# A fused transformer block: products ahead of the transposes, weights in chunks, gated dummy matmuls, and TensorE's branch behind its last matmul

## The chip, the cores and the metric

The kernel runs on one core of one Trainium2 chip. The metric is the device time of one execution in microseconds. The span of a profile (first to last instruction) is some 1.7 us shorter than that time. All executions here scatter by about 1 us, as much as the effects in question, so most comparisons rest on five executions of a kernel and on the runs of the kernel before that were taken beside them on the same chip.

## The reference

```python
mod = (silu(c) @ w_mod).reshape(c.shape[0], 6, 1, -1)        # c: 1x512, w_mod: 512x3072
sa, ca, ga, sb, cb, gb = (mod[:, i] for i in range(6))
h = layernorm(x) * (1 + ca) + sa                              # x: 1x2048x512
x = x + ga * attention(h, k_cache, v_cache, wq, wo)           # 32 heads of 128, 8 kv heads, last 512 keys
h = layernorm(x) * (1 + cb) + sb
x = x + gb * (relu(h @ w1) @ w2)                              # 512 -> 1792 -> 512
```

The rows are worked in four blocks of 512. Before the first score matmul the kernel needs the first block normalized, transposed, scaled with `1 + ca` and shifted with `sa`, and projected to queries.

## The kernel before

The start, cut to what the change touches. The dummy matmuls (`warm`) produce nothing that is used; they are meant to bring TensorE's clock up. In the trace of before the clock is read from spacing: its dummies start 427 ns apart, and 512-column matmuls in the body 216 ns (508 to 513 us). The first is called half clock here.

```python
    for i in range(2):                                   # x: two halves, one per queue
        dma(x_sb[:, 2 * i:2 * i + 2, :], ..., eng=ACT if i else SP)
    dma(c_row[:, :], ...)
    load_wm01(0)                                         # modulation weights: two halves of 512 KB
    load_wm01(1, ACT)
    load_wq(0, 2, ACT)                                   # query weights, heads 0 and 1
    load_wq(2, 2)
    load_k(0)
    load_v(0)
    ...
    warm(7)                                              # dummies, 128x512
    silu_exp(5)                                          # transpose of c on TensorE, exp on ScalarE
    warm(9)
    ...                                                  # statistics of row tile 3 on ScalarE
    silu_mul()                                           # GpSimd: 1/(1+exp(-c)), times c
    ln_stat(0); ln_stat(1); rstd_add(0, 2); rstd_pow(0, 2)    # powers on GpSimd
    ln_stat(2); rstd_add(2, 3); rstd_pow(2, 4)
    ln_norm(0); ln_norm(1)                               # VectorE
    ...                                                  # row tile 3 normalized on GpSimd, after the powers
    ln_tposes(0, TB[0])                                  # 4 transposes of row tile 0
    for f in mod_cols_mm(0, QBK): f()                    # the 32 products with one column
    ln_norm(2)
    mod_cols_evac(0, QBK)                                # modc, on VectorE
    for tl in range(1, TPB):
        ln_tposes(tl, TB[tl // 2])
    ...                                                  # scale and shift, first projections
```

The end. A flag, computed at about 478 us, tells whether a general version of the kernel must be run instead. Each engine loads it and branches at its own place; TensorE does so before two of the groups of the second MLP product:

```python
                mlp.insert(len(mlp) - 2, lambda: cut_here("pe"))
    ...
                kb.emit(stream, e, 0, n_ops)             # n_ops: the cut
                e.wait_ge(sems[flag_ev[0]], flag_ev[1])
                v = e.value_load(flag[0:1, 0:1])
                with e.If(v != 128):
                    ...                                  # rest of the fast version, then the general version
                with e.Else():
                    kb.emit(stream, e, n_ops)            # rest of the fast version
```

## Time and profile before

| | before |
|---|---|
| time, median of the first three runs | 560.52 us (560.2 to 560.57) |
| span of the profile | 559.4 us |
| TensorE busy | 98% |
| transpose of c | 4.94 us |
| products | 9.04 to 9.98 us |
| first projection | 10.86 us |
| first scores (first record at 13.34; the one ahead of it has none) | about 13.12 us |
| TensorE's branch | 510.64 to 514.08 us |
| last matmul's start to the end of the span | 2.89 us |

The profiled execution took 561.1 us, 0.6 us more than that median.

Busy time by engine, from the first part of the page, gives the frame: no engine but TensorE is near its limit.

```profile
PE 550.5 (98%) x4060; PEld 315.8 (56%) x4134; DVE 253.8 (45%) x551; ACT 348.9 (62%) x453; POOL 54.7 (10%) x53
```

### The profile page before, as it was taken

To read this page: it belongs to the slowest core of one execution; us is meant where nothing else is said; L and a number is where in the kernel's file an instruction comes from. 1 tells how busy PE (TensorE), PEld (TensorE's weight loads), DVE (VectorE), ACT (ScalarE), POOL (GpSimd) and SP (SyncE) were. 2 spreads that over 40 slices of the span, in tenths; PEclk is the share of its full clock that TensorE was granted. 3 is DMA by queue.
4 is the path that set the end of the run, shared out by engine and by line. 5 is a ranking of instruction groups with operands and counts; after the bars stand their busy time and mean duration, and the time that the engine had idled before them with its cause. 6 is when DMAs were issued, how large, how long until landed. Compare 5 with 4: busy or idle time off the path is not lost.

```text
span 559.4 us, 9666 instructions
## 1 busy us (share of the span) xinstructions
PE 550.5 (98%) x4060; PEld 315.8 (56%) x4134; DVE 253.8 (45%) x551; ACT 348.9 (62%) x453; POOL 54.7 (10%) x53
## 2 busy tenths in 40 slices
PE   8999999999999999999999999999999999999998
PEld 4665555555555555555555555555555654444444
DVE  4455555553546544335445443333354448321134
ACT  4986666666666666666666666666666644432500
POOL 3000022004410000033000000332000000000000
DMA  9897763513114144352352412111215110210001
GB/s 268 248 207 174 143 169 46 114 39 76 40 38 76 39 73 117 58 133 57 94 95 57 76 40 39 39 39 38 39 39 76 39 30 0 44 34 23 22 29 47
DMA packets 113309, 42.67 MB, mean 76 GB/s; under 512 B 93928, under 2 KB 112104, under 8 KB 113256
## 3 DMA queue, kind: packets, MB, share of 16 engines
q1 hardware_dynamic: 112024, 40.82, 34.3%
q10 hardware_dynamic: 1232, 1.15, 0.6%
q8 instruction: 33, 0.54, 0.4%
q14 instruction: 20, 0.16, 0.1%
HBM read 18.35 MB, written 2.10 MB: 37 GB/s over the span
## 4 chain that ended last, share of the span: by engine, by line
PE 98%; issue 1%; DMA 1%; DVE 0%; SPq 0%; DVEq 0%
PE psS L1372 28%; PE psO L1372 27%; PE psQ L1372 23%; PE psW L1372 20%; DMA c_row<-in_c_dram 1%; DVE qT L1611 0%; DVE hT L1630 0%; SPq L1303 0%; DVE PT L1723 0%; DVE PT L1725 0%; PE psS L1375 0%; PE psO L1416 0%; DVE modc L1438 0%; DVEq L123 0%
## 5 line engine op out<-in xcount | busy, mean ns | idle before, releaser
L1493 ACT ACTIVATE PT<-psS 128x1024 bf16<-128x1024 f32 x256 | 262.7, 1028 | 128.2 <-PE psS L1372 128.1
L1372 PE MATMUL psS<-qT,kT 128*128 128x512 bf16 x508 | 150.9, 379 | 0.5 <-DVE qT L1611 0.4
L1372 PEld LDWEIGHTS psO<-v,PT 128*128 128x128 bf16 x2048 | 126.6, 98 | 30.2
L1372 PE MATMUL psO<-v,PT 128*128 128x129 bf16 x2048 | 137.0, 220 | 0.0
L1372 PE MATMUL psQ<-hT,wq 128*128 128x512 bf16 (+1 forms) x510 | 130.5, 377 | 0.3 <-DVE hT L1630 0.2
L1503 DVE RECIPROCAL rinv<-psO 128x4 f32<-128x4 f32 x128 | 23.3, 182 | 227.2 <-PE psO L1372 227.2
L1372 PE MATMUL psW<-wo,oT 128*128 128x512 bf16 x454 | 118.1, 379 | 3.0
L1504 DVE TENSOR_TENSOR o<-psO,rinv 128x512 bf16<-128x512 f32 x128 | 88.5, 691 | 4.9 <-DVE rinv L1503 0.5
L1372 PEld LDWEIGHTS psQ<-hT,wq 128*128 128x128 bf16 x512 | 49.9, 98 | 60.3 <-issue 0.6
L1372 PEld LDWEIGHTS psS<-qT,kT 128*128 128x128 bf16 x512 | 49.5, 98 | 58.9 <-ACT PT L1493 0.7
L1485 ACT ACTIVATE qT<-psQ 128x512 bf16<-128x512 f32 x126 | 74.7, 593 | 0.0
L1712 ACT ACTIVATE wq<-psS 128x512 bf16<-128x512 f32 x56 | 33.4, 597 | 49.3 <-PE psS L1372 48.9
L1372 PEld LDWEIGHTS psW<-wo,oT 128*128 128x128 bf16 x512 | 45.0, 98 | 32.9 <-DVE acc L1526 1.2
L1526 DVE TENSOR_TENSOR acc<-psW,acc 128x512 f32<-128x512 f32 x48 | 33.2, 691 | 6.5 <-PE psW L1372 6.5
L1372 PE MATMUL psO<-wmw,wq 128*128 128x512 bf16 (+1 forms) x165 | 32.8, 352 | 0.3
L1529 POOL TENSOR_TENSOR acc<-acc,gaf 128x512 f32<-128x512 f32 x12 | 15.6, 1303 | 146.7 <-DVE acc L1526 139.8
L1388 POOL TENSOR_TENSOR rstd<-rstd,cst 128x4 f32<-128x4 f32 x7 | 7.2, 1025 | 216.8 <-DVE rstd L1387 216.8
L1723 DVE TENSOR_TENSOR PT<-psO,gbf 128x512 f32<-128x512 f32 (+1 forms) x12 | 7.5, 624 | 40.4 <-PE psO L1372 40.4
L1372 PE MATMUL psS<-h2T,wmw 128*128 128x512 bf16 x109 | 25.0, 379 | 0.2
L1372 PEld LDWEIGHTS psO<-wmw,wq 128*128 128x128 bf16 x168 | 15.3, 98 | 16.5
L1372 PE MATMUL psS<-hT,wmw 128*128 128x512 bf16 x110 | 24.4, 379 | 0.1
L1382 DVE BATCH_NORM_STATS2 st<-x 128x6 f32<-128x512 bf16 x31 | 21.1, 681 | 4.8 <-DMA x<-in_A_x_dram 4.8
(85 smaller groups left out, 192.6 us busy)
## 6 DMA issues: line engine op xcount, KB each, us to landing
wo<-in_A_wo_dram SPq DMA_DIRECT2D x4, 1024.0 KB, 5.9
wq<-in_A_wq_dram SPq DMA_DIRECT2D x7, 512.0 KB, 4.6
wmw<-in_B_w_dram SPq DMA_DIRECT2D x14, 256.0 KB, 3.1
wmw<-in_w_mod_dram SPq DMA_DIRECT2D x5, 512.0 KB, 4.8
oT<-o SPq DMA_TRANSPOSE x128, 2.4
out_dram<-PT SPq DMA_DIRECT2D x15, 128.0 KB, 1.7
x<-in_A_x_dram SPq DMA_DIRECT2D x3, 512.0 KB, 4.3
v<-in_A_v_cache_dram SPq DMA_DIRECT2D x8, 128.0 KB, 3.8
```

The costliest lines, as they stand in the source:

```text
L1372: kb.op(PE, lambda e: e.matmul(out_ap, lhsT, rhs, start=start, stop=stop), reads=reads, group_writes=[R_b[k] for k in bk], signal=signal)
L1382: kb.op(DVE, lambda e: e.bn_stats(st[:, t, :], x_sb[:, t, :]), reads=[R_x[t]], writes=[R_st[t]])
L1388: kb.op(POOL, lambda e: e.tensor_tensor(rstd[:, sl], rstd[:, sl], cst[:, 0:1].to_broadcast([P, hi - lo]), op=ALU.pow), reads=R_rstd[sl] + ...
L1485: kb.op(ACT, lambda e: e.activation(qT[u % NQT][:, :], bank[bk], ACTF.Copy), reads=[R_b[bk]], writes=[R_qT[u % NQT]])
L1493: kb.op(ACT, lambda e: e.activation(PT[u % NPT][:, pr * 2:pr * 2 + 2, :], s_ps[pr][:, :, :], ACTF.Exp, scale=scale), reads=[R_b[pr * 2], R ...
L1503: kb.op(DVE, lambda e: e.reciprocal(rinv[:, u, :], o_ps[:, :, P]), reads=[R_b[5], R_b[6]], writes=[R_rinv])
L1504: kb.op(DVE, lambda e: e.tensor_tensor(o_sb[u % NOS][:, :, :], o_ps[:, :, 0:P], rinv[:, u, :].unsqueeze(2).to_broadcast([P, TPB, P]), op=A ...
L1526: kb.op(DVE, lambda e: e.tensor_tensor(acc[:, tl, :], bank[WBK], acc[:, tl, :], op=ALU.add), reads=[R_b[WBK], R_acc[tl]], writes=[R_acc[tl]])
L1529: kb.op(eng, lambda e: e.tensor_tensor(acc[:, tl, :], acc[:, tl, :], gaf[:, :], op=ALU.mult), reads=[R_acc[tl], R_ga], writes=[R_acc[tl]])
L1712: kb.op(ACT, lambda e: e.activation(h1T[b % 2][:, fc, :], bank[bk], ACTF.Relu), reads=[R_b[bk]], writes=[R_h1[b % 2][fc]], pre=all_events( ...
L1723: kb.op(DVE, lambda e: e.tensor_tensor(yt[i][:, c0:c1], bank[bk][:, c0:c1], gbf[:, c0:c1], op=ALU.mult), reads=[R_b[bk], R_gb], writes=[R_ ...
```

## The change

The intent: run the 32 products as soon as silu(c) is there, ahead of all transposes; let their weights come in the order of use; replace nine dummies, which hold TensorE back until 8.8 us, with a few that wait for events; and save TensorE's stall at the branch by taking the branch when TensorE has nothing left to do. The diff, cut to its core:

```diff
-        c0, c1 = i * DC // 2, (i + 1) * DC // 2
-        dma(wm01[:, c0:c1, :], wm01v[:, c0:c1, :], f"wm{i}", writes=[R_wm[i]], eng=eng)
+        dma(wm01[:, i, :], wm01v[:, i, :], f"wmc{i}", writes=[R_wmc[i]], eng=eng)
...
-    load_wm01(0)
-    load_wm01(1, ACT)
-    load_wq(0, 2, ACT)
+    for i in range(DC):
+        load_wm01(i, (ACT, SP)[i % 2])
+    for i, eng in enumerate((SP, SP)):
+        dma(wq_sb[:, 2 * i:2 * i + 2, 0:QA * Dh], ..., f"wqa{i}", writes=[R_wqa[i]], eng=eng)
+    load_k(0)
     load_wq(2, 2)
-    load_k(0)
     load_v(0)
-    kb.op(POOL, lambda e: e.memset(ones[:, :], 1.0), writes=[R_ones])
+    kb.op(DVE, lambda e: e.memset(ones[:, :], 1.0), writes=[R_ones])
...
-    warm(7)
+    warm(10)
     silu_exp(5)
-    warm(9)
...
     ln_stat(0)
+    warm(3, [R_mv[0]])
     ln_stat(1)
+    warm(2, [R_mv[1]])
...
-    ln_tposes(0, TB[0])
     fs = mod_cols_mm(0, QBK)
     for f in fs:
         f()
+    ln_tposes(0, TB[0])
+    mod_cols_evac(0, QBK)
     ln_norm(2)
-    mod_cols_evac(0, QBK)
...
-    for tl in range(1, TPB):
-        ln_tposes(tl, TB[tl // 2])
+    ln_tposes(1, TB[0])
+    warm(2, bk=6)
+    ln_tposes(2, TB[1])
+    ln_tposes(3, TB[1])
+    warm(1, bk=6)
...
-                mlp.insert(len(mlp) - 2, lambda: cut_here("pe"))
...
+    cut_here("pe")
```

More of the change, by code (lines that the diff above doesn't have):

```diff
@@ L1319, in build_fast @@
     R_q1 = RL("q1_", 2)
+    R_wmc = RL("wmc", DC)
+    R_wqa = RL("wqa", 2)
     R_cf, R_m01 = Res("cf"), Res("m01")
@@ L1350, in load_wm01 @@
     def load_wm01(i, eng=None):
-        c0, c1 = i * DC // 2, (i + 1) * DC // 2
-        dma(wm01[:, c0:c1, :], wm01v[:, c0:c1, :], f"wm{i}", writes=[R_wm[i]], eng=eng)
+        dma(wm01[:, i, :], wm01v[:, i, :], f"wmc{i}", writes=[R_wmc[i]], eng=eng)
     def wm_res(sl, cc):
-        return R_wm[cc // (DC // 2)] if sl < 2 else R_wm[sl]
+        return R_wmc[cc] if sl < 2 else R_wm[sl]
     def load_wo(j):
@@ L1363, in load_mlp @@
         if not wm_done:
-            wm_done.extend(all_events(R_wm))
+            wm_done.extend(all_events(R_wm + R_wmc))
         f0 = i % (FC // 2) * 2
@@ L1375, in tpose, with warm @@
         kb.op(PE, lambda e: e.transpose(out_ap, in_ap, ident[:, :]), reads=list(reads) + [R_ident], group_writes=[R_b[k] for k in bk], signal=signal)
-    def warm(n):
+    def warm(n, gate=(), bk=7):
         for i in range(n):
-            mm(bank[WBK], ones[:, :], ones[:, 0:1].to_broadcast([P, QB]), True, True, [R_ones], [WBK], i == n - 1)
+            mm(bank[bk], ones[:, :], ones[:, 0:1].to_broadcast([P, QB]), True, True, [R_ones] + list(gate), [bk], i == n - 1)
     def ln_stat(t):
@@ L1480, in q_mms @@
             mm(bank[bk], wq_sb[:, cc, h * Dh:(h + 1) * Dh], hT[b % 2][:, cc, :], i == 0, i == DC - 1,
-               [R_wq[h], R_hT[b % 2][cc]] + ([R_h0[cc]] if b == 0 else []), [bk], i == DC - 1)
+               (R_wqa if h < QA else [R_wq[h]]) + [R_hT[b % 2][cc]] + ([R_h0[cc]] if b == 0 else []), [bk], i == DC - 1)
         q_evac(u, bk)
@@ L1561, in build_fast @@
     dma(c_row[:, :], c[0].rearrange("(c p) -> c p", p=P), "c", writes=[R_c])
-    load_wm01(0)
-    load_wm01(1, ACT)
-    load_wq(0, 2, ACT)
+    for i in range(DC):
+        load_wm01(i, (ACT, SP)[i % 2])
+    for i, eng in enumerate((SP, SP)):
+        dma(wq_sb[:, 2 * i:2 * i + 2, 0:QA * Dh], wqv[:, 2 * i:2 * i + 2, 0:QA * Dh], f"wqa{i}", writes=[R_wqa[i]], eng=eng)
+    load_k(0)
     load_wq(2, 2)
-    load_k(0)
     load_v(0)
-    kb.op(POOL, lambda e: e.memset(ones[:, :], 1.0), writes=[R_ones])
+    kb.op(DVE, lambda e: e.memset(ones[:, :], 1.0), writes=[R_ones])
     kb.op(POOL, lambda e: e.memset(cst[:, 0:1], -0.5), writes=[R_cst])
@@ L1636, in q_half @@
             mm(bank[bk][:, hf * HB:(hf + 1) * HB], wq_sb[:, cc, u * Dh:(u + 1) * Dh], hT[0][:, cc, hf * HB:(hf + 1) * HB], cc == CC_ORDER[0], cc == CC_ORDER[-1],
-               [R_wq[u], R_half[hf][cc]], [bk], cc == CC_ORDER[-1])
-    for tl in range(1, TPB):
-        ln_tposes(tl, TB[tl // 2])
+               [R_wqa[cc // 2], R_half[hf][cc]], [bk], cc == CC_ORDER[-1])
+    ln_tposes(1, TB[0])
[3 more added lines that the diff above has]
+    warm(1, bk=6)
     mod_half(0, 0, DVE)
@@ L1712, in h1_group @@
         kb.op(ACT, lambda e: e.activation(h1T[b % 2][:, fc, :], bank[bk], ACTF.Relu), reads=[R_b[bk]], writes=[R_h1[b % 2][fc]],
-              pre=all_events(R_wq) if b < 2 else ())
+              pre=all_events(R_wq + R_wqa) if b < 2 else ())
     def y_group(b, tl, c0=0, c1=D, deng=None):
```

## The prediction

> **What bounds the kernel now.** I read three views in this order. First the shares by engine of the chain that ended last, for the whole span:
>
> ```profile
> PE 98%; issue 1%; DMA 1%; DVE 0%; SPq 0%; DVEq 0%
> ```
>
> TensorE is the path for all but some 2% of 559.4 us, so nothing that shortens work on another engine in the body of the kernel can help. What is left is where TensorE is on the path without useful work, or waits: the first 13 us, and single stalls. So second, the same chain in order of time for the first 14 us (start, us, what):
>
> ```profile
> 1.24 3.66 DMA c_row<-in_c_dram
> 4.90 0.05 issue
> 4.95 0.18 PE psO L1416
> 5.13 3.86 PE psW L1372 x9
> 8.98 0.22 PE psS L1375 x4
> 9.21 0.79 PE psQ L1372 x32
> 10.00 0.02 issue
> 10.02 0.18 DVE modc L1438
> ...
> 10.30 0.42 DVE hT L1630
> ...
> 10.86 0.78 PE psQ L1372 x4
> 11.64 0.89 PE psO L1372 x8
> ...
> 12.55 0.44 DVE qT L1611
> ```
>
> The reader is to see the third to fifth PE pieces: nine dummy matmuls hold TensorE until the first transposes, then the 32 modulation products run, then their eviction on VectorE (10.02), and only then can the transposed rows be scaled (10.30), the queries projected (10.86) and scored (about 13.1; the first score matmul has no record). From there TensorE never waits for long, so what is won before it should arrive whole at the end.
>
> Third, what the other engines were doing meanwhile, in the timeline:
>
> ```profile
> 5.06 3.92 PE L1372 MATMUL psW<-ones 128*128 128x512 bf16 x9
> ...
> 6.92 0.20 POOL L1423 TENSOR_TENSOR sc_bf<-c_f,tmp 128x4 bf16<-128x4 f32 x1
> 7.08 1.51 POOL L1591 TENSOR_TENSOR rstd<-rstd,cst 128x2 f32<-128x2 f32 x2
> ...
> 7.82 1.22 DVE L1393 TENSOR_SCALAR xn<-x,mv,rstd 128x512 bf16<-128x512 bf16 x3
> ...
> 8.70 0.90 POOL L1604 TENSOR_SCALAR xn<-x,s,rstd 128x512 bf16<-128x512 bf16 x1
> ```
>
> The products' vector sc_bf is ready at 7.12, but the products start at 9.04: 1.9 us late. Their weights are part of that: by the completion events in the trace, the two halves of the modulation weights landed at 6.15 and 7.91 (the half that is needed first came last). The normalized rows are there at about 8.23, 8.55, 9.04 (VectorE) and 9.60 (GpSimd), the last one being at the end of a serial GpSimd chain that starts with the transposed c.
>
> In the tail TensorE takes the data-dependent branch between two groups of matmuls. The records of sequencer instructions, which the views leave out, give a flag load at 510.09 and a compare-and-branch from 510.64 to 514.08 (3.44 us). TensorE had about 18 matmuls queued, so only this is lost:
>
> ```profile
> 513.09 0.53 PEld L1372 LDWEIGHTS psO<-wmw,wq 128*128 128x128 bf16 x3
> 514.14 0.76 PEld L1372 LDWEIGHTS psQ<-wmw,wq 128*128 128x128 bf16 x5 [0.52 <-issue]
> ```
>
> From matmul to matmul the gap is 408 ns where 216 is usual: 0.19 us lost.
>
> [...] all sixteen dummies here are 427 ns apart, up to 8.44 us, and the transposes after 8.8 are 56 ns apart. [...] the 32 one-column products took 0.78 us from 9.04, 25 ns each[...]. [...] GpSimd, with nothing else to do, branched at 478.85 and reached its next instruction at 481.89, 3.0 us later.
>
> **The change, part by part.**
>
> (a) Weights in four chunks. The modulation weights come as four transfers in the order of use, two per queue; the first query weights (two heads) follow instead of sharing the ACT queue. The bytes are the same. Packets moved at about 190 KB per half microsecond from 3 us on; x and the four chunks are 1.57 MB, which the packets in the trace reach at about 6.5. I estimate the first two chunks by 5.7 and the last by 6.9, in place of 7.91. The two-head query weights are another 256 KB at 160 KB per half microsecond: about 7.8, needed at 10. The keys and the next query weights come by about 9 and 10, needed at 12. None of these binds.
>
> (b) Products ahead of the transposes, nine dummies after c replaced by three and two that wait for the statistics. Products start when sc_bf is there: 7.12 plus any delay of c. Ten dummies now stand before the transpose of c instead of seven: from about 1.0 they take 0.40 + 9 x 0.427 = 4.24 us at half clock, to about 5.24, against a start of 4.95 now. So c slips by up to 0.3 us, less if the clock is released meanwhile; I take 0.2. Products then run from 7.4 to 8.2, off the path; their eviction follows the second normalization on VectorE at about 8.8, against 10.02.
>
> (c) What the path becomes. The first projection stands in TensorE's order behind all transposes and one dummy. The last row tile comes from GpSimd: 9.60 + 0.2 = 9.80. Transposes from 9.85, four at 56 ns, then a dummy of 216 ns: the first projection at about 10.29, against 10.86. Its four matmuls, at 109 ns, no longer wait for the ScalarE half (that wait costs about 0.17 us now), so the next projection starts at 10.73 against 11.48: 0.75 us won. The second half of the scaling on VectorE starts at about 10.3 against 10.95, three steps of 0.32 and one wait of 0.40 give 11.34, in time for the third projection, which ends at about 11.6 against 12.35. From there the evictions and the first scores follow as now, 0.75 us earlier, at about 12.4. Without the slip of c it would be 0.95.
>
> (d) The branch moved behind TensorE's last matmul. It gives back the 0.19 us. But the branch now sits at the end. TensorE's sequencer finished issuing at 555.54 (its final drain started there); the flag load and the step to the branch take 0.56, so the branch starts at 556.10 of the old clock, and with a fetch of 3.0 (GpSimd) to 3.44 (TensorE) and a drain of about 0.1 it is done at 559.2 to 559.65. The last drain of the other engines is at 559.15, after the last output landed. So the end slips by 0.05 to 0.5; I take 0.4.
>
> Sum: -0.75 - 0.19 + 0.40 = -0.54 us, and 560.52 - 0.54 = 560.0.
>
> **The rivals.** *The clock does not come up in time.* [...] products, transposes and projections run at half speed; the sixteen projection matmuls alone would cost 16 x 0.109 = 1.7 us more. [...] In executions where it happens the kernel would be at 560.5 to 561.5; I give it one in five.
> *The start was not on the path as the profile has it.* Dummies at half clock are what hold the transposes now; in executions where the clock is released sooner, the before kernel loses less, and the gain shrinks to 0.3 us. The three times before differ by 0.37 us, which fits such a jitter. That makes 560.3.
> *The branch is free at the end.* If the 3.44 us was mostly the wait for queued matmuls and not the fetch, it ends under the last transfers, and the sum becomes -0.94: 559.6. GpSimd's 3.0 us speaks against it.
> *A transfer binds.* If the two-head query weights or the keys came 1 us after they are needed, the gain in (c) would be gone: 560.7. The landing estimates leave 2 us.
>
> **Range and chances.** The parts span from -0.95 - 0.19 + 0.05 = -1.1 to a cold clock at +0.5; with 0.2 us of scatter between runs I take 559.2 to 560.8. All of these are under 0.25% of the time, while 2% would be 11 us: within 2% is all but certain.
>
> **What would show it.** Products before transposes, at 7.2 to 7.5; the eviction of modc near 8.8; first projection at about 10.3 and first scores at about 12.4; at 514 us an unbroken row of matmuls (216 ns); at the end TensorE's branch and a drain after 559 us of the old clock, the span ending with it and not with the last output. Wrong would be: first scores before 12.0 or after 12.8, transposes 107 ns apart (cold clock), a wait for wq or kT, or a TensorE that is done before the last output lands.

The sum stands as -0.75 - 0.19 + 0.40 = -0.54 us, so 560.0 us. No run here shows what makes the clock come up, so the one in five is my bare estimate. What the trace shows: spacings of 427, 56 and 25 ns, and GpSimd's 3.0 us. For the branch it also shows a 16 KB instruction block, from 511.63 to 512.65, inside its 3.44 us; this is the fetch of the texts below.

## More of the kernel before

One line of the DMA view: the last two small outputs, 32 KB each, with the time from issue to landing in the last column.

```profile
out_dram<-PT SPq DMA_DIRECT2D x1, 32.0 KB, 1.5
out_dram<-PT ACTq DMA_DIRECT2D x1, 32.0 KB, 1.5
```

## The result

The changed kernel takes 561.29 us in the median of five runs (560.93 to 562.69), the kernel before 560.2 us (559.97 to 560.57). The ratio is 1.0023, with a 95% interval of 1.0009 to 1.0038: slower by about 1 us, though within 2%. Here and below a ratio is the mean time of one kernel's runs over the mean of the other's of the same rounds, so it is not quite the ratio of the medians.

The profiled execution of the changed kernel is the slowest of its five (562.69 us). Its span is 560.9 us. It is compared here with the profile of before, an execution of 561.1 us; neither is the median of its kernel. Three places account for the difference:

| | before | changed | difference |
|---|---|---|---|
| first product of probabilities and values starts | 16.68 us | 17.72 us | +1.04 |
| from there to the last matmul's start | 539.79 us | 539.59 us | -0.20 |
| from the last matmul's start to the end of the span | 2.89 us | 3.56 us | +0.67 |
| span | 559.36 us | 560.87 us | +1.51 |

**The middle** went as intended. The change took the branch away from between the groups, and the weight loads stand without a hole where the profile of before showed one (timeline of the changed kernel, TensorE's weight loads; start, duration, group):

```profile
513.27 1.39 PEld L1373 LDWEIGHTS psO<-wmw,wq 128*128 128x128 bf16 x7
514.78 0.31 PEld L1373 LDWEIGHTS psQ<-wmw,wq 128*128 128x128 bf16 x2
```

**The start** is the next view, the chain in order of time in the changed kernel (start, duration, what):

```profile
1.10 4.45 PE psW L1373 x10
5.55 0.13 PE psO L1417
...
6.34 1.06 POOL tmp L1423
...
8.83 0.93 PE psS L1376 x8
...
11.89 0.80 PE psQ L1373 x4
...
14.17 0.59 PE psS L1373 x2
```

Two things are new. Ten dummies now stand on the path ahead of c: c had landed at 4.69, and its transpose starts at 5.48. And the transposes, at 8.8 to 11.4, take very long. Why is seen in busy time by stretch. A line has the stretch, its length, the busy us (and instructions) of PE, PEld, DVE, ACT and POOL, and then TensorE's granted clock, the DMA share and GB/s:

```profile
5.67:9.08 3.41, 2.65 (x41) 1.46 (x41) 2.50 (x9) 2.16 (x8) 2.94 (x5) 1.00 1.11 237
9.08:12.50 3.42, 3.20 (x21) 2.32 (x20) 2.23 (x8) 1.58 (x3) 0.95 (x2) 0.50 1.18 289
```

The clock is granted from 5.67 (the records begin there; before it the dummies stand 427 ns apart, so it was half), and is halved again from 9.08 to 12.50, just when the transposes and the first projections run. The 2.65 us of busy time in the stretch before overstate it, since the ends of matmuls are modelled: a transpose's record lasts 0.22 us where transposes stand 56 ns apart. The columns streamed there are five dummies of 216 ns, four transposes of 56 ns and 32 single columns, by estimate from these spacings about 1.3 of 3.41 us. So in this execution the clock was taken back after a stretch that was less than 40% full. The other profiles agree. Thirteen have clock records. Count 216 ns for 512 columns, and cut the time from the grant on into stretches of 3.413 us, the length of each of the two clock records above: in the first 15 us, four stretches were followed by half a clock (here, in e3, e7 and e11), and these held 0.36 to 0.38 of their length in streamed columns. No stretch there that kept the clock held less than 0.44 (e1). But for the changed kernel this is one execution: of the five, only this one has a mean clock of 0.997, and the other four (0.999 to 1.0) are slower than the kernel before as well. One caution holds for every mean clock below: since the records begin with the grant, a clock that comes up late doesn't lower the mean (e13: granted at 9.52, mean 1.0). The profile of before has no clock record at all, so its mean is 1.0 while its dummies stand 427 ns apart.

**The end**: the last outputs take longer to land than in the kernel before.

```profile
out_dram<-PT SPq DMA_DIRECT2D x1, 32.0 KB, 2.7
out_dram<-PT ACTq DMA_DIRECT2D x1, 32.0 KB, 2.1
```

The records of sequencer instructions, which the views leave out, show TensorE's flag load at 556.38, its branch from 557.16 to 560.52 (3.35 us), and its drain from 560.58 to 560.65. SyncE, which waits for the outputs, drains at 560.61. The two are level at the end.

### The profile page after: what moved, and what is told of

It reads as the page before. It is cut to its first block, busy times and chain, and to the rows that moved or that the text cites. A ratio compares the mean times of both kernels' runs of the same rounds, so it can differ in the third digit from the quotient of the medians. Undisturbed runs are those within 1.5% of the kernel's fastest.

```text
span 560.9 us, 9675 instructions
## 1 busy us (share of the span) xinstructions
PE 551.4 (98%) x4062; PEld 316.7 (56%) x4136; DVE 254.0 (45%) x552; ACT 349.1 (62%) x453; POOL 54.6 (10%) x52
## 4 chain that ended last, share of the span: by engine, by line
PE 98%; issue 1%; POOL 0%; DVE 0%; ACT 0%; POOLq 0%
PE psS L1373 28%; PE psO L1373 27%; PE psQ L1373 22%; PE psW L1373 20%; PE psS L1376 0%; POOL tmp L1423 0%; POOL rstd L1592 0%; DVE qT L1614 0%; DVE xn L1394 0%; DVE PT L1729 0%; DVE PT L1731 0%; POOL tmp L1422 0%; PE psW L1376 0%; POOL sc_bf L1424 0%; DVE ones L1570 0%
```

## The experiments

Twelve runs were made, of eleven kernels, all correct, in three groups on three chips (the number e6 is not used). The time beside each is its median; the median of before in the same group was 560.46, 560.56 and 560.25 us.

### e1: the branch put back, and e2: the branch alone

```diff
 # e1: the changed kernel
+                mlp.insert(len(mlp) - 2, lambda: cut_here("pe"))
...
-    cut_here("pe")
```

> The changed kernel with TensorE's branch put back between two groups of matmuls. Theory (the branch at the end costs): in the changed kernel's profile the time from TensorE's last matmul to the end of the span grew by 0.67 us and 0.19 us were saved in the middle, so this should be about 0.5 us faster than the changed kernel, a ratio to before of about 1.0015, and the end after the last matmul should be back at about 2.6 us, ended by the last output. Rival (the branch is free, all of the loss is at the start): same as the changed kernel, 1.002 to 1.0025.

e1 took 560.79 us, ratio 1.0002 (0.9989 to 1.0015). With the branch back, most of the loss is gone: 0.33 us are left of 1.09 in the medians. The changed kernel was not run again beside e1, and the two intervals overlap, so the times alone don't prove it. The profiles do: the end after the last matmul is back at 2.87 us, and it is 2.87 to 2.90 us in all eleven profiles with the branch in the middle, 3.30 to 4.00 us in the three with it at the end.

e2 is the opposite edit on the kernel before: the line at the cut removed, `cut_here("pe")` behind everything.

> The kernel before with only TensorE's branch moved behind its last matmul. Theory (the fetch after the branch ends later than the last output, and the output itself may land later): slower by 0.3 to 0.6 us, ratio 1.0005 to 1.001, the profile ends with TensorE's branch of about 3.4 us. Rival (the branch is free at the end): faster by 0.19 us, 0.9997.

e2 took 561.52 us, ratio 1.0018 (1.0005 to 1.0031): slower by 1.06 us in the medians, more than the 0.3 to 0.6 us that I had expected. The profile's end after the last matmul is 4.00 us instead of 2.89. The branch lasts from 555.33 to 559.13, 3.79 us, and the last outputs are later still:

```profile
out_dram<-PT SPq DMA_DIRECT2D x1, 32.0 KB, 3.2
out_dram<-PT ACTq DMA_DIRECT2D x1, 32.0 KB, 2.5
```

The completion events say how. The last output has sixteen completions. Fifteen came by 557.88 and the sixteenth at 558.94; for the output before it, fifteen by 557.07 and one at 558.79. In the profile of before all sixteen came within 0.17 us. Among the DMA packets there is one new one here: a 16 KB instruction block, from 556.35 to 557.76, inside TensorE's branch. The data packets show what it did. Each of these two outputs moves in 128 packets of 256 bytes. Of SyncE's output 120 had started by 556.70, and the other eight, one sixteenth, start from 557.75 on, as the block ends; of ScalarE's, 120 had started by 557.50 and the last eight follow those of SyncE from 558.00. In the changed kernel the block ends at 559.19 and the eight start at 559.19. So the block that is fetched during the branch stands in front of one sixteenth of the last outputs. The branch at the end costs twice, once on TensorE and once in the transfer, and the two run level.

### e9: the branch at the end, its flag loaded early

To take the two costs apart in time, the flag's load into a register was left where the branch stood before, while the branch stays at the end. That is 224 matmuls ahead of it by the count of the trace (load at 509.36 us, branch at 554.61); the "some 90" of the expectation is wrong.

```diff
 # the kernel before; "pe" is cut behind everything, as in e2
-                mlp.insert(len(mlp) - 2, lambda: cut_here("pe"))
+                mlp.insert(len(mlp) - 2, lambda: cut_here("pe_load"))
...
-                kb.emit(stream, e, 0, n_ops)
+                kb.emit(stream, e, 0, n_load)
                 e.wait_ge(sems[flag_ev[0]], flag_ev[1])
                 v = e.value_load(flag[0:1, 0:1])
+                kb.emit(stream, e, n_load, n_ops)
```

> The kernel before with the branch behind TensorE's last matmul, as in e2, but the flag loaded some 90 matmuls earlier. Theory (at the end the chain of load, fetch and drain on TensorE and the instruction fetch [...] set the end together): the branch starts 0.7 us earlier, the fetch is over before the last output is issued, so its sixteen completions come together, and the end after the last matmul is 2.9 to 3.4 us instead of 4.0: ratio to before 0.9995 to 1.0005. Rival (the output is late for another reason, or the fetch takes longer than the tail whatever): stays at 1.0015.

It took 560.57 us, ratio 1.0003 (0.9989 to 1.0017), and the end after the last matmul was 3.30 us: 0.7 us of e2's loss came back for the 0.8 us by which the branch starts earlier. The fetch now hits one output earlier in the row, 64 KB from the ACT queue, which takes 2.9 us where e2 and the kernel before have 1.6:

```profile
out_dram<-PT ACTq DMA_DIRECT2D x1, 64.0 KB, 2.9
out_dram<-PT SPq DMA_DIRECT2D x1, 32.0 KB, 2.5
out_dram<-PT ACTq DMA_DIRECT2D x1, 32.0 KB, 1.9
```

My expectation that the last completions would come together was wrong: one was still 0.41 us late. The delay moves with the fetch: the block ends at 557.00, and eight of the 128 packets of the 64 KB output start from 556.99 on, the others by 556.34. So in all three profiles with the branch at the end a 16 KB block (1.0 to 1.4 us) is followed by one late completion of sixteen, 0.41 to 1.06 us behind the others for the last of them, and in none of the others.

### e7 and e10: the branch in the middle, its flag loaded early

The same trick where the branch stood before: load the flag two groups of 14 matmuls ahead of it. (The expectation says 56 matmuls; the edit and the trace make it 28.)

```diff
 # the kernel before
                 mlp.insert(len(mlp) - 2, lambda: cut_here("pe"))
+                mlp.insert(len(mlp) - 5, lambda: cut_here("pe_load"))
```

> The kernel before with TensorE's load of the flag into a register 56 matmuls earlier than its branch; the branch stays. Theory (flag load of 0.5 us and fetch of 3.4 to 3.8 us together are just longer than the 3.9 us of matmuls that TensorE has queued, so 0.2 to 0.5 us are lost): the row of matmuls behind the branch is unbroken, 0.2 to 0.45 us faster than before, ratio 0.9993. Rival (the branch waits for the queue to drain, whatever the load does): a gap of about 0.4 us from matmul to matmul stays, ratio 1.0.

e7 took 560.22 us against 560.56, ratio 0.9994 (0.998 to 1.0007). In its profile the way from the first value product to the last matmul is 539.59 us, as short as with no branch there at all.

> The kernel of e7 again, for a firmer number on the version that looks faster than both: ratio to before 0.9992 to 0.9998 if the 0.2 to 0.45 us of the branch are won in every run; 1.0 if e7's 0.9994 was chance.

The repeat took 560.09 us against 560.25, ratio 0.9997 (0.9984 to 1.0011). In its profile the branch lasted 3.96 us, longer than in any other, and 0.16 us were lost after all. Ten executions in two groups are 0.34 and 0.16 us below the medians of before. Both intervals hold 1.0, so the gain is likely and not proven. It is the best version that came out, and its medians lie below those of the kernel before that was run beside it.

### e3: the gated dummies alone

```diff
 # the kernel before
     silu_exp(5)
-    warm(9)
...
     ln_stat(0)
+    warm(3, [R_mv[0]])
     ln_stat(1)
+    warm(2, [R_mv[1]])
```

> The kernel before with only the nine dummies after c replaced by the three and two that wait for the statistics. Theory (the clock[...]): the clock is not released, or taken back, before the projections, so the transposes stand 107 ns apart and the first scores come 0.5 to 2 us later than 13.1; ratio 1.001 to 1.003, scattered from run to run. Rival (the clock is not the cause; what holds the start is the order and the dummies): the transposes can start at 8.25 instead of 8.82, the time is the same or 0.5 us shorter, 0.999 to 1.0.

It took 561.43 us, ratio 1.0018 (1.0006 to 1.003). Three of its six executions have a mean clock of 0.997 or 0.994. The profile shows the same pattern as that of the changed kernel, with the stretches at another time:

```profile
4.85:8.27 3.42, 1.65 (x9) 0.50 (x10) 3.22 (x10) 2.16 (x8) 2.78 (x5) 1.00 1.10 354
8.27:11.68 3.41, 3.41 (x54) 3.06 (x53) 2.32 (x8) 1.53 (x4) 1.04 (x2) 0.50 1.26 261
```

So without the nine dummies a stretch is left that holds 0.36 of its length in columns, and the clock is halved right behind it. With the gated ones in their place the clock is lost more often, in three of six executions (two of 29 of the kernel before, below). But that is not all of e3's loss: its three executions with a mean clock of 0.999 or 1.0 took 561.01, 561.73 and 561.98 us, no less than the other three (560.85, 561.12 and 562.59). What slowed those is not shown; a clock that came up late would not be seen in the mean. The kernel before isn't free of it, either: of its 29 runs in the three groups, two have 0.997, and took 561.82 and 561.86 us, some 1.5 us over the medians of their groups.

### e4: the holes filled

e1, with three more dummies behind the gated ones and a 128-column dummy after every fourth product.

```diff
 # e1
     warm(2, [R_mv[1]])
+    warm(3)
...
-    for f in fs:
+    for i, f in enumerate(fs):
         f()
+        if i % 4 == 3 and i < len(fs) - 1:
+            mm(bank[6][:, 0:P], ones[:, :], ones[:, :], True, True, [R_ones], [6], False)
```

> The branch put back as in e1, and TensorE's holes filled: three more dummies behind the gated ones and a 128-column dummy after every fourth product. Theory (the clock): [...] the throttling at about 9 us stays away in most runs; first scores at about 12.6 to 13.0, 1.0 us earlier than in the changed kernel; ratio to before 0.9985 to 1.0, and 0.8 us or so faster than e1. Rival (the clock doesn't matter, the serial chain from c does): the same as e1 or slower by the added dummies.

By estimate from the spacings (216 ns for a dummy, 56 ns for 128 columns) the added work would bring the columns of the changed kernel's stretch from 5.67 to 9.08 from about 1.3 to 2.3 of its 3.41 us. The time was 560.94 us, ratio 1.001 (0.9998 to 1.0022): not faster than e1. None of its six executions shows a lowered clock, but none of e1's five does, either. With the branch back there was no loss of clock to cure in these executions, as far as the mean shows. (One of the six took 562.32 us with a span of only 559.4, so its extra 1.2 us lies outside the span.) The clock explains the profiled execution of the changed kernel; that it explains the median is not shown.

### e5 and e8: seven dummies before c

```diff
 # e1
-    warm(10)
+    warm(7)
     silu_exp(5)
+    warm(3)
```

> As e1 (changed start, branch back in the middle), with three of the ten dummies moved behind the transpose of c, so seven stand before it as in the kernel before. Theory (c has landed at 4.5 to 4.9, but in the changed kernel it waits for ten dummies until 5.48, and the serial GpSimd chain behind it sets the last normalized rows and so the first scores): c is transposed at 4.5 to 4.9, everything up to the first scores is 0.6 to 0.9 us earlier than in e1, first scores at about 12.0; about 559.9 to 560.2, ratio to before 0.999. Rival (the start is bound elsewhere, by weights or the clock[...]): within 0.2 us of e1, 1.0002, with throttled windows in some runs.

A miss: 560.59 us, ratio 1.0004 (0.999 to 1.0017), against e1's 1.0002. The profile itself showed what I had expected (c at 4.50, first scores at 12.02 instead of e1's 12.73), but the times don't keep it.

> e5 and e7 together: the changed start with seven dummies before c, the branch in the middle with its flag loaded early. If both theories hold the gains add: 559.5 to 559.9, ratio to before 0.998 to 0.999, faster than both kernels. If only the branch theory holds: 560.3.

e8 has the same start, and took 560.23 us, ratio 0.9998 (0.9984 to 1.0011). Its profile tells why the start is no sure win. Here the clock came up at 7.05 and not at 5.83, so the dummies behind c took until 7.6; then half of the products waited for a chunk of weights (timeline of e8; in brackets the idle time and its releaser):

```profile
7.64 0.76 PE L1373 MATMUL psQ<-sc_bf,wmw 128*128 128x1 bf16 x16
8.57 0.73 PE L1373 MATMUL psQ<-sc_bf,wmw 128*128 128x1 bf16 x16 [0.17 <-DMA wmw<-in_w_mod_dram]
```

First scores: 12.78. Of the second chunk fifteen completions had come by 6.08 and the last at 7.99; the third chunk's last came at 8.52, and the fourth's at 8.90.

### e11, e12, e13: the parts of the start alone

e11 is the kernel before with `warm(10)` before c and `warm(6)` behind it.

> The kernel before with ten dummies before the transpose of c and six behind it, instead of seven and nine. Theory (the wait of c behind dummies lengthens the serial GpSimd chain, which sets the first projection about 0.5 us after the last normalized rows): c is transposed at about 5.45 instead of 4.5 to 4.9, last rows at 10.1, first projection at about 10.65, first scores at about 12.75 to 12.9; 0.3 to 0.6 us slower than before, ratio 1.0005 to 1.001. Rival (the chain has slack): first scores at about 12.35 as in the fast starts of the kernel before, ratio 1.0.

561.37 us, ratio 1.0016 (1.0002 to 1.0029): slower by 1.12 us, more than the 0.3 to 0.6 that I had expected. Its profile doesn't show the reason that I gave. There the clock came up at 3.8, so c was not delayed (4.66), and the loss came from a throttled stretch from 10.64 to 14.06. What slowed the other four stays open.

e12 is the kernel before with the change's loads only.

> The kernel before with only the loads of the change: modulation weights in four chunks, the first two heads' weights in two, keys ahead of the next weights. Theory (the chunks don't bring the last weights earlier, 7.7 to 8.9 against 7.8 to 8.0, because single completions of a chunk come late; and the products aren't on the path): the same as before, ratio 0.9997 to 1.0005, products at about 8.3. My prediction's step (a): last chunk at 6.9. A late chunk as in e8 would give a start up to 0.6 us later in some runs.

560.39 us, ratio 1.0005 (0.9991 to 1.0018): no gain. Its last chunk landed at 8.56 (the kernel before: 7.91), its products started at 8.20, and the first projection at 10.02.

e13 is the kernel before with only the products and their eviction moved ahead.

> The kernel before with only the products ahead of the first transposes and their eviction ahead of the third normalization. Theory (GpSimd's last rows set the first projection, the products don't): products at about 8.0, eviction at about 9.0, but the first projection stays at about 10.1 where the clock comes up in time; ratio 0.9995 to 1.0005. Rival (the prediction's view, the products and their eviction are on the path): first scores 0.7 us earlier than in the fast starts of the kernel before, 11.6; ratio 0.9985.

560.47 us, ratio 1.0003 (0.999 to 1.0017): no gain. In its profile the clock came up late, at 9.52, so its times within the start (first projection 10.87) aren't to be compared with fast starts.

### What the start of the kernel before really is

e2 has the same start as the kernel before, instruction for instruction, and so have e7, e9 and e10. Their profiles are four more samples of it. This is the chain in e2:

```profile
0.79 3.92 DMA x<-in_A_x_dram
...
4.74 0.71 DVE st L1382
...
7.65 0.33 DVE xn L1393
...
8.03 0.40 PE psS L1375 x4
8.42 0.78 PE psQ L1372 x32
...
10.08 0.78 PE psQ L1372 x4
```

The dummies aren't on it. The arrival of x, the statistics and the first normalized tile are, and the transposes follow the tile by 0.06 us. c landed at 4.45 here and the clock came up at 6.31; in the profile that I predicted from, 4.90 and about 8.7 (dummies 427 ns apart up to 8.45, transposes 56 ns apart from 8.82). First scores are at 12.34 (e2), 12.39 (e9) and 12.28 (e10), not at 13.12; e7 fell in a throttled start (13.45). The profile of before was a slow start of its kernel. The timed runs say so for more than four samples: 22 of the 29 executions of the kernel before in the three groups have spans of 558.3 to 558.8 us, and the profile that I predicted from has 559.4.

## Why the prediction was wrong

The prediction was 560.0 us, 0.5 us faster; measured was 561.29, 1.1 us slower in the medians. So the forecast of the change was off by 1.6 us (-0.54 against +1.09). As far as medians of different groups can be set against each other, 1.1 of this is the start (-0.75 forecast, +0.33 in e1) and 0.55 the branch (+0.21 forecast, middle and end together; +0.76 from e1 to the changed kernel). By its own steps:

**What bounds the kernel now: right for the body, wrong for the start.** It read "nine dummy matmuls hold TensorE until the first transposes" as the kernel's bound. That was so in the one profiled execution. In the four other samples of the same start the dummies were off the path, and in three of them the first scores came some 0.75 us earlier. This is the first step that failed: the 0.75 us that the change was to win was there only in the slow start that had been profiled. The rival "the start was not on the path as the profile has it" had this, and was given too little weight. (Its own sum was also off: 560.52 - 0.3 - 0.19 + 0.40 is 560.4, not 560.3.) That the profiled execution was slow could be known beforehand: 561.1 us, where three others took 560.2 to 560.57.

**(a), the chunks: wrong.** The last chunk was put at 6.9. It landed at 8.34 in the changed kernel and at 7.7 to 8.9 in the five other profiles with chunks, where the halves landed at 7.7 to 8.4 in eight profiles. The estimate took the mean rate of the bytes; what counts is the last of sixteen completions (in e8 the second half of the products starts at 8.57, the third chunk's last completion is at 8.52). In the changed kernel the first of them came at 6.82 and the last 1.5 us later; in e8 one came 1.9 us after the fifteenth. e12 shows no gain from the loads.

**(b), the delay of c: mechanism right, size wrong.** 0.2 us was taken; c started 0.54 us later than in the profile of before, and 0.80 us after it had landed. The ten dummies started at 1.10 and ran at half clock (427 ns apart) to the end.

**(c), the path of the start: close where the clock held, but against the wrong reference.** First scores were put at 12.4; they are at 12.73 in e1, where the clock held. In the profiled execution of the changed kernel two of the prediction's signs of being wrong stood: first scores at 14.17, and transposes 107 ns apart from 10.40 on. Against the fast starts of before (12.28 to 12.39) this is no gain but a loss of some 0.4 us. e1's 0.33 us in the medians agrees, but its interval holds 1.0. e13 shows no gain from moving the products, and the low end of its interval (0.999, or -0.56 us) excludes 0.75 us: in the fast starts the first projection follows products, statistics and the last normalized rows almost together. In e10 the last rows from GpSimd are ready at 9.48, their transposes start at 9.53 and 9.71 is the last, while the last product starts at 8.98 and the first projection starts at 10.02. Nothing there had 0.75 us of slack. (One sum of the step is misworded: three steps of 0.32 and one of 0.40 from 10.3 would end at 11.66. The 11.34 counts two of 0.32 and a last one of 0.40, as in the trace.)

**(d), the branch: mechanism right, size wrong, and this is most of the loss.** The 0.19 us of the middle came (0.20). The end was to slip by 0.4 and slipped by 0.67 in the changed kernel and by 1.11 in e2 (2.89 to 4.00). From the flag's load to the branch it took 0.78 us and not 0.56; the branch itself took 3.35 in the changed kernel, within the 3.0 to 3.44, and 3.79 in e2. And one cost was not in the sum at all: the instruction block stands ahead of one sixteenth of the last outputs (eight of 128 packets in e2). e1 and e2 show it from both sides: 1.0023 falls to 1.0002 when the branch goes back, and the branch alone makes 1.0018, clear of noise.

**The rivals.** "The branch is free at the end" was rightly doubted. "The clock does not come up in time" did happen, in that it was lost again: it stands in e3's profile (clock 0.50 from 8.27 to 11.68), and is the profiled execution of the changed kernel (0.50 from 9.08 to 12.50). But it is one in five, as said, and is not shown for the median. "A transfer binds" came nearer than I had thought: the projection's own weights landed at 9.28, ahead of their use, but chunks of the modulation weights held the products in e8.

**What stays open.** Why e11 lost 1.1 us while e1, with the same ten dummies, lost 0.3; and why single completions of a chunk come so late. The parts don't add up, either: branch (1.06 us), gated dummies (0.97) and ten dummies first (1.12) would each explain the whole loss. That the costs of the start interact through the clock, which was halved from 8.27 on in e3, from 9.08 in the changed kernel and from 10.64 in e11, is likely and not shown; only the branch is separated cleanly, since it lies 500 us away from the rest.

## What to carry to other kernels

One profile is one sample. If an effect of a microsecond is predicted from the first ten microseconds, look at several profiles of the same start before deciding what bounds it. TensorE's branch held it for 3.35 to 3.96 us in every profile (on the four other engines the record of the branch lasts 50 to 72 ns). In the middle, the engine's queued work hid all but 0.13 to 0.48 us, and with the register loaded earlier all but 0 to 0.16 us; behind the last instruction nothing hid it, and its fetch also delayed the outputs that the end waits for. Here the clock was lost after stretches that held 0.36 to 0.38 of their length in columns and kept at 0.44 and more: gated dummies left such a stretch in e3, and too many dummies ahead of a small serial chain put themselves on the path (c landed at 4.69 and was transposed at 5.48).
